# ScalarE's order at the end of the first chunk, and sums and splits made sooner in the second layer, in an adaLN block with a long convolution and a token-mixing MLP

## The chip, the cores and the metric

The kernel runs on one core of a Trainium2 chip. A core has five engines that work at the same time, each through its own list of instructions in order: TensorE (PE in the profile; its weight loads are PEld), VectorE (DVE), ScalarE (ACT), GpSimd (POOL) and SyncE (SP), which here only issues transfers. They meet through semaphores. TensorE writes to PSUM, which TensorE, VectorE and ScalarE reach; the rest of the data on the chip lies in SBUF.

The metric is the device time of one execution in microseconds. Three executions of the kernel before took 678.05, 681.57 and 681.95 us, with a median of 681.57. A fourth, profiled, took 683.93.

## The reference

One batch entry, 2048 tokens, 640 channels, all float32. A condition vector gives six modulation rows of 640. The block has two residual parts. The first normalises each token, modulates it, and multiplies it with the output of a depthwise path: a short causal convolution of `k`, a product with `v`, and a causal convolution as long as the sequence. The second normalises again and runs an MLP over the token axis.

```python
mod = (silu(c) @ w_mod).reshape(1, 6, 1, 640)
sa, ca, ga, sb, cb, gb = mod[:, 0], ..., mod[:, 5]

h = layernorm(x) * (1 + ca) + sa
kv = short_conv(k, shift_k) * v                  # 4 taps, causal, per channel
y = long_conv(kv, ssm_k) + kv * ssm_D            # 2048 taps, causal, per channel (by FFT)
x = x + ga * (h * y)

h = layernorm(x) * (1 + cb) + sb                 # (2048, 640)
u = gelu(einsum("bsd,sf->bdf", h, w1) + b1)      # w1: (2048, 1728)
y = einsum("bdf,fs->bds", u, w2) + b2            # w2: (1728, 2048)
x = x + gb * transpose(y)
```

## The kernel before, in words

**Depthwise path.** The 640 channels are five chunks of 128. For each chunk the long convolution is a two-step transform done as matmuls: `step1` (line 223) forward, on the filter side and on the data side; `f2` (line 242), the second forward step in eight groups, each followed by a ScalarE copy to `kt` (line 246) and two VectorE products (`p`), whose sums GpSimd writes to `Y`; `i2` (line 271) and `i1` (line 291) back. `gate` multiplies the result into the modulated, normalised tokens `A1` on VectorE and adds the product to the tokens on GpSimd.

The work is ordered by hand: the order of the program's lines is the order on each engine. While a chunk is in `f2`, ScalarE also makes the first factors of that chunk, `A1 = x * rstd - mean * rstd`, one activation for each of 16 token groups (the list `ac`, line 298), and VectorE fills its gaps with the short convolution of the chunk after (`kv_ops`, the list `fill`). Chunk 0 is different: the token statistics and the modulation are made at its end, so its 16 factors stand there, after the statistics' square roots (`rstd`, line 335).

**The end of chunk 0** (lines 606 to 637). The modulation's first three rows are a product of `silu(c)` with `w_mod` in five blocks (`mod_part`, line 351) into the PSUM tile `tap`. ScalarE copies the sum to SBUF (`mod_sum`, line 355). TensorE spreads each of three rows over all partitions (`mod_row`, line 362). ScalarE evicts rows 0 and 1 to `G0` and `G1` (lines 369 and 371) and VectorE multiplies row 2 into both. `k0` is ScalarE's eviction of the last `step1` group (line 229). The PSUM tiles of this part turn over three slots, in the order in which they are asked for: row 0, row 1 and row 2 take the slots of the last `i2`'s two tiles and of the last `step1`; the two `i1` tiles take those of rows 0 and 1. Then VectorE applies `G1` and `G0` to the factors (`po`, in two halves, each a multiplication and an addition), ScalarE permutes the next chunk's filter (`perm`, line 168, in two halves), and GpSimd does a quarter of chunk 2's short convolution (`kv_ops(1, pool)`) before the two additions of `gate`.

**First MLP layer.** Weights are split into a high part of a reduced float32 type (`fp32r`, written by ScalarE) and a low rest (VectorE); each product is three matmuls, high by high, high by low, low by high.

**Second MLP layer.** The first four of the 16 output blocks are done plainly (line 1123). The other twelve go in six pairs (`NP = 6`), each pair by seven products in place of eight (a Strassen-Winograd scheme) over the seven combinations

```python
ORDER = ("A11", "A12", "S1", "S2", "S3", "S4", "A22")
```

For the product numbered `n` (7 in a pair, 42 in all): `sums(n)` makes its weight combination on VectorE; it does something only for S1 (one addition), for S2 (two subtractions, which make S3 as well) and for S4 (one). `split(n)` writes the high half on ScalarE (line 1034) and the low half on VectorE into one of three slots, `slots[n % 3]`. `product(n)` is 21 matmuls of 320 columns (line 1046), three for each of seven blocks; the third of each three uses the low half. `outcome(n)` combines the products and, for most, finishes an output half (`finish`: a SCALAR_TENSOR_TENSOR from PSUM, line 1053 or 1055, and one or two TENSOR_TENSOR, then a transfer out). The products' PSUM tiles turn over four slots, which the four plain blocks `acc[0]` to `acc[3]` filled before; `acc[0]` and `acc[1]` are emptied early (`early`, line 1097), `acc[2]` and `acc[3]` by four calls of `finish` in the loop at `n == 1`. The loop (lines 1136 to 1155) runs two splits ahead of the products.

VectorE's and GpSimd's TENSOR_TENSOR instructions all have the line of a helper, 57.

Of the kernel before, what the change touches and what calls it, by code (L numbers as in the profile page):

```python
# [47 lines left out]
def mixer_kernel(ctx: ExitStack, tc: tile.TileContext, q, k, v, shift_k, ssm_k, ssm_D, w1, b1, w2, b2, c,  # L48
# [123 lines left out]
    def taps():  # L172

        act.activation(TAP, TR.rearrange("p (i s) -> p s i", s=4), AF.Copy)
# [183 lines left out]
    def mod_row(i, t, slot=None, later=False):  # L358

        ps, j = psum(slot).rearrange("p (h m) -> p h m", h=2), i % 3  # L360
        for h in range(2):
            pe.matmul(ps[:, h, 0:320], ones[32 * j:32 * j + 1, 0:1].to_broadcast([1, 128]),
                      t[32 * j:32 * j + 1, 320 * h:320 * h + 320], start=True, stop=True)
        ps = ps[:, :, 0:320]
        two = lambda t: t.rearrange("p (h m) -> p h m", h=2)
        if later:
            return lambda: act.activation(two(GB), ps, AF.Copy)
        if i == 0:
            act.activation(two(G0), ps, AF.Copy)
        elif i == 1:  # L370
            act.activation(two(G1), ps, AF.Copy, bias=1.0)
        elif i == 2:
            TT(dve, two(G0), ps, two(G0), ALU.mult)
            TT(dve, two(G1), ps, two(G1), ALU.mult)
        elif i == 3:
            act.activation(two(SB), ps, AF.Copy, accum_out=msb)
        elif i == 4:
            dve.tensor_scalar(two(CB), ps, 1.0, None, op0=ALU.add)
# [98 lines left out]
    def run(ops):  # L477
        for f_ in ops:
            f_()
# [69 lines left out]
    for c in range(NC):  # L549
        cn = c + 1 if c + 1 < NC else None  # L550
        ac, po = a1_ops(c)
# [42 lines left out]
        if c == 0:  # L594
            for kk in range(2, 5):
                mod_load(0, kk, homes[kk])
            step1(0, 0)
            ps = psum()
            pe.transpose(ps[:, 0:36], stg, ID[0:36, 0:36])
            act.activation(cols, ps[:, 0:36], AF.Copy)  # L600
            act.activation(sil, cols[:, 30:35], AF.Silu)
            step1(0, 1)
            i2(0)
            step1(0, 2)
            i2(1)
            k0 = step1(0, 3, True)
            for kk in range(4):
                mod_part(tap, kk, pl[kk])
                if kk == 2:
                    load_D(1)  # L610
                    load_ks(1)
            rstd(rs1, nm1, 0, 16)
            run(ac[0:8])
            k0()
            mod_part(tap, 4, pl[4])
            for o, i in ((0, 2048), (64, 2048)):
                dve.tensor_scalar(T_v1[o:o + 64, i:i + 2048], T_v1[64:128, 0:2048], 1.0, None, op0=ALU.mult)
            dve.tensor_scalar(T_v1[64:128, 0:2048], T_v1[0:64, 0:2048], 1.0, None, op0=ALU.mult)
            load_halo(2)
            load_k(2, 0, n=2)  # L620
            load_v(2, 0, n=2)
            load_k(2, 2, n=2)
            load_v(2, 2, n=2)
            mod_sum(tap, T_kt[:, 0:640])
            run(ac[8:16])
            pool.tensor_scalar(PW, TR.rearrange("p (i s) -> p s i", s=4), 1.0, None, op0=ALU.mult)
            perm_add(1)
            run(kv_ops(1, pool))
            for i in range(3):
                mod_row(i, T_kt[:, 0:640])  # L630
            taps()
            load_taps(3)
            run(po[0:2])
            perm(1)
            load_D(2)
            load_ks(2)
            fill.extend(kv(3, ((0,), (2, 1), (3,))))
        elif cn is not None:
            for t in range(2):
                step1(0, t)  # L640
            perm(cn)
            if c + 2 < NC:
                fill.extend(kv(c + 3 if c + 3 < NC else None))
            else:
                fill.extend(x1s(cc, j) for cc in range(c) for j in range(16))
        else:
            blk.update({f: (j16(t[:, 0:2048]), j16(t[:, 2048:4096])) for f, t in (
                (0, mem("w0", 4096, "wb0")), (1, mem("w1", 4096, "wb1")))})
            mod_load(3, 3, T_z[:, 0:1920])
            mod_load(3, 4, P[:, 0:1920])  # L650
            for kk in range(3):
                mod_part(tap, kk, pl[kk])
            t = mem("in", 4288, "wb3")
            blk[3] = j16(t[:, 0:2048]), j16(t[:, 2048:4096])
            split_rows(0, X, (0, 1, 3))
            split_rows(1, T_aux[:, 0:2048], (0, 1, 3))
            run(po)
# [353 lines left out]
    def sums(n):  # L1011

        p, w_ = n // 7, ORDER[n % 7]
        if p >= NP:
            return
        a = lambda k: A[p, k]
        if w_ == "S1":
            A[p, w_] = S1
            TT(dve, S1, a("A21"), a("A22"), ALU.add)
        elif w_ == "S2":  # L1020
            TT(dve, a("A21"), a("A11"), a("A21"), ALU.subtract)
            TT(dve, a("A11"), S1, a("A11"), ALU.subtract)
            A[p, "S3"], A[p, "S2"] = a("A21"), a("A11")
        elif w_ == "S4":
            TT(dve, a("A12"), a("A12"), a("S2"), ALU.subtract)
            A[p, "S4"] = a("A12")
# [74 lines left out]
    for s in range(NW):  # L1101
        i = NF + s
        acc.append(psum().rearrange("p (h m) -> p h m", h=2))
        split_w(i)
        load_w(i + 1)
        if s < 3:
            t_ops(3 + s)
        if s > 1:
            early(s - 2)
        if s == 3:  # L1110
            load_pair(1, 0, 3)
            m_w.append(mem("w1", 4096, "m_w0"))
            slots += [(q7(m_w[0], 1792 * i), q7(m_w[0], 1792 * i + 896)) for i in range(2)]
            split(0)
            split(1)
            sums(2)
            sums(3)
        wh, wl = blk[i]
        for f_ in range(NF):
            u = U[f_]  # L1120
            for k, (w, r) in enumerate(((wh, 0), (wh, 2), (wl, 0))):
                for h in range(2):
                    pe.matmul(acc[s][:, h, 0:320], w[:, f_].bitcast(F32R), u[r + h].bitcast(F32R),  # L1123
                              start=f_ == 0 and k == 0, stop=f_ == NF - 1 and k == 2)
# [9 lines left out]
    t_ops(6, pool)  # L1134
    load_pair(1, 3, 4)
    for n in range(7 * NP):
        if n:
            sums(n + 3)
        split(n + 2)
        product(n)  # L1140
        if n == 1 or n == 3:
            outcome(n - 1)
        if n != 0 and n != 2:
            outcome(n)
        if n == 1:
            for k in range(4):
                finish(2 + k // 2, k % 2, acc[2 + k // 2][:, k % 2, 0:320], (o2, o4, o3, o1)[k], xq[4 + k])
        if n == 2:
            x_pair(1)
        if n % 7 == 6:  # L1150
            load_pair(n // 7 + 2)
            x_pair(n // 7 + 2)
# [34 lines left out]
```

## Time and profile before

| | |
|---|---|
| timed runs | 678.05, 681.57, 681.95 us; median 681.57 |
| profiled execution | 683.93 us, of which span 682.1 |
| TensorE busy | 629.4 us (92%), weight loads 598.4 |
| VectorE busy | 498.3 us (73%) |
| ScalarE busy | 300.2 us (44%) |
| GpSimd busy | 133.9 us (20%) |
| mean granted TensorE clock | 0.975 |

The stretches in the trace: up to about 103 us chunk 0 and the next chunk's filter; chunks 1 to 4 to about 280; the second normalisation, overlapped with the first products, to about 344; the first MLP layer to 495; the second layer's plain blocks to 544.4; the six pairs to the end.

A row of a timeline has the start in us, the length in us, engine, line, operation, output and inputs by tile name, the shape of the output and of the input, and the count of instructions merged. In square brackets stands how long the engine sat idle just before and what released it. A table by stretch has, after the stretch and its length, the busy time of PE, PEld, DVE, ACT and POOL, each with the count of instructions, then the granted TensorE clock (1.00 is full), the transfers' share of the DMA engines, and GB/s.

### The profile page before, as it was taken

Reading aid. Unit: us, or ns where it says so; the run is one execution under the profiler, and the core shown is the slowest. Engines: PE = TensorE matmul, PEld = TensorE weight load, DVE = VectorE, ACT = ScalarE, POOL = GpSimd, SP = SyncE. Lnnn points to the kernel's source line nnn. Section 1 sums busy time; section 2 is a strip of 40 time slices with the busy share of each in tenths; the row PEclk is TensorE's granted clock in tenths of the full one; section 3 lists DMA queues with packets and bytes.
Section 4 is the critical chain, followed back from the end, with each engine's and each line's share of the span. In section 5 each row is a group of like instructions: output and inputs, shape, how many; then the busy total and the mean of one; then the engine's idle time right before and its main releaser. Section 6 shows DMA issues by size and latency. Waiting matters only on the chain.

```text
span 682.1 us, 20757 instructions
## 1 busy us (share of the span) xinstructions
PE 629.4 (92%) x9119; PEld 598.4 (88%) x9119; DVE 498.3 (73%) x869; ACT 300.2 (44%) x483; POOL 133.9 (20%) x157
## 2 busy tenths in 40 slices
PE   6878778999999898798899999999999989999997
PEld 2877568899989897688899889999999989999997
DVE  7789589989898279798866622321689779888995
ACT  1654655646657265457654222322344133333331
POOL 6762067226134142000000000000000520000000
PEclk9998989999999799888899999999999999999999
DMA  9999797375426153440308333335441634355601
GB/s 188 219 260 274 246 179 157 91 138 121 66 65 215 35 134 104 91 97 1 62 1 154 62 63 63 62 64 115 120 136 55 197 114 124 102 167 166 184 32 38
DMA packets 166538, 81.23 MB, mean 119 GB/s; under 512 B 90830, under 2 KB 156912, under 8 KB 166448
## 3 DMA queue, kind: packets, MB, share of 16 engines
q1 hardware_dynamic: 159276, 78.32, 47.5%
q10 hardware_dynamic: 6916, 1.31, 1.1%
q8 instruction: 71, 1.16, 0.7%
q0 software_dynamic: 256, 0.28, 0.2%
q14 instruction: 19, 0.16, 0.1%
HBM read 69.40 MB, written 10.49 MB: 117 GB/s over the span
## 4 chain that ended last, share of the span: by engine, by line
PE 68%; DVE 14%; ACT 6%; DMA 5%; issue 3%; SPq 2%; POOL 1%; ACTq 0%; POOLq 0%; DVEq 0%
PE pst L445 20%; PE pst L1046 17%; PE pst L1123 7%; PE pst L223 7%; PE pst L242 6%; PE pst L271 5%; PE pst L291 3%; DVE p L57 3%; ACT z L280 2%; DMA in<-in_w_mod_dram 1%; PE pst L919 1%; DVE tap L57 1%; DMA y<-in_A_ssm_k_dram 1%; DVE sm L548 1%; DVE kt L57 1%
## 5 line engine op out<-in xcount | busy, mean ns | idle before, releaser
L242 PE MATMUL pst<-z,w 128*64 128x64 f32 x2560 | 78.4, 223 | 13.1 <-DVE p L57 6.7
L242 PEld LDWEIGHTS pst<-z,w 128*64 128x64 f32 x2560 | 76.4, 138 | 15.6 <-issue 9.1
L229 ACT ACTIVATE z<-pst 128x1024 f32<-128x1024 f32 (+2 forms) x45 | 43.1, 977 | 46.3 <-PE pst L223 46.2
L57 POOL TENSOR_TENSOR y<-p 128x256 f32<-128x256 f32 x72 | 51.3, 741 | 42.4 <-DVE p L57 42.1
L57 DVE TENSOR_TENSOR p<-pst,kt 128x512 f32<-128x512 f32 x80 | 50.7, 680 | 7.9 <-ACT kt L246 7.9
L1046 PE MATMUL pst<-r_z,m_w 128*128 128x320 f32 x222 | 42.0, 312 | 2.2 <-DVE m_w L57 2.2
L882 ACT ACTIVATE pst<-pst,sm 128x640 f32<-128x640 f32 x13 | 10.0, 767 | 75.9 <-PE pst L445 75.9
L271 PEld LDWEIGHTS pst<-v,y 32*128 32x128 f32 x1280 | 38.2, 187 | 5.4 <-issue 4.8
L271 PE MATMUL pst<-v,y 32*128 32x64 f32 x1280 | 40.1, 272 | 2.5 <-issue 2.3
L246 ACT ACTIVATE kt<-pst 128x512 f32<-128x512 f32 x40 | 24.0, 599 | 34.6 <-PE pst L242 18.7
L1034 ACT ACTIVATE m_w<-m_v 128x896 fp32r<-128x896 f32 x24 | 22.7, 951 | 36.9 <-PE pst L1046 16.8
L223 PE MATMUL pst<-v,x 128*64 128x128 f32 x512 | 34.6, 291 | 4.5 <-issue 4.0
L223 PE MATMUL pst<-v,p 128*64 128x128 f32 x640 | 36.7, 274 | 0.8 <-ACT p L168 0.8
L1046 PEld LDWEIGHTS pst<-r_z,m_w 128*128 128x128 f32 x222 | 35.2, 190 | 2.4 <-DVE m_w L57 2.4
L57 POOL TENSOR_TENSOR m_p<-u_i,r_z 128x320 f32<-128x320 f32 x1 | 0.9, 875 | 183.4 <-issue 183.4
L223 PEld LDWEIGHTS pst<-v,p 128*64 128x64 f32 x640 | 34.8, 137 | 2.1 <-ACT p L168 1.7
L57 DVE TENSOR_TENSOR tap<-tap,kt 128x512 f32<-128x512 f32 x51 | 35.5, 696 | 1.3
L223 PEld LDWEIGHTS pst<-v,x 128*64 128x64 f32 x512 | 31.1, 147 | 5.8 <-issue 5.2
L291 PEld LDWEIGHTS pst<-z,v 64*64 64x64 f32 x1280 | 23.9, 156 | 9.1 <-issue 3.8
L280 ACT ACTIVATE z<-pst 128x512 f32<-128x512 f32 x38 | 20.9, 647 | 23.3 <-PE pst L271 23.3
L291 PE MATMUL pst<-z,v 64*64 64x64 f32 x1280 | 25.3, 241 | 6.3 <-issue 2.4
L57 DVE TENSOR_TENSOR kt<-in,tap 128x512 f32<-128x512 f32 x42 | 28.8, 685 | 1.2
(308 smaller groups left out, 1507.4 us busy)
## 6 DMA issues: line engine op xcount, KB each, us to landing
x<-in_B_w_dram SPq DMA_DIRECT2D x20, 512.0 KB
m_x<-xs SPq DMA_DIRECT2D x28, 160.0 KB
out_dram<-m_x SPq DMA_DIRECT2D x28, 160.0 KB
aux<-in_A_ssm_k_dram SPq DMA_DIRECT2D x8, 512.0 KB
m_v<-in_B_w_dram SPq DMA_DIRECT2D x9, 448.0 KB
in<-in_w_mod_dram SPq DMA_DIRECT2D x4, 960.0 KB
x<-in_B_w_dram SPq DMA_DIRECT2D x7, 448.0 KB
in<-in_A_v_dram SPq DMA_DIRECT2D x22, 128.0 KB
```

The lines of the kernel that those rows point to most:

```text
L57: TT = lambda eng, o, a, b, op: eng.tensor_tensor(o, a, b, op=op)
L223: pe.matmul(ps[64 * ri:64 * ri + 64, o:o + 255:2], lhs, F1[:, 128 * ri:128 * ri + 128], start=True, stop=True)
L229: act.activation(Z[:, side, t, :, k0:k1], ps.rearrange("p (a k e) -> p a k e", a=4, e=2)[:, :, k0:k1], AF.Copy)
L242: pe.matmul(ps[64 * h:64 * h + 64, o:o + 64], W2[k1 // 32][:, 2 * (k1 % 32) + ri], rhs, start=True, stop=True)
L246: act.activation(kt.rearrange("p (m i) -> p m i", i=32), pv[:, :, 1], AF.Copy)
L271: pe.matmul(pp[qd // 2][:, o:o + 64], Y[p, ri, i:i + 2].rearrange("p i k -> p (i k)"), V2[p, 64 * ri:64 * ri + 64], start=ri == 0, stop=ri ...
L280: act.activation(o, i, AF.Copy)
L291: pe.matmul(ps[64 * b:64 * b + 64, 512 * e + 64 * jj:512 * e + 64 * jj + 64], V1[p, ri, n2], T2[p, :, 32 * ri + n2], start=ri == 0, stop=r ...
L445: pe.matmul(ps[0:m, h, 0:320], w_.bitcast(F32R), r_[:, 320 * h:320 * h + 320].bitcast(F32R), start=first and i == 0, stop=last and i == 2)
L1034: act.activation(W[n][0].bitcast(F32R), A[p, w_], AF.Copy)
L1046: pe.matmul(bank[n], w[:, i].bitcast(F32R), r.bitcast(F32R), start=i == 0 and k == 0, stop=i == 6 and k == 2)
L1123: pe.matmul(acc[s][:, h, 0:320], w[:, f_].bitcast(F32R), u[r + h].bitcast(F32R), start=f_ == 0 and k == 0, stop=f_ == NF - 1 and k == 2)
```

## The change

At the end of chunk 0, ScalarE's list is reordered. Before: eight factors, the `step1` eviction `k0`, the copy of the modulation's sum, eight factors, the evictions of rows 0 and 1. After: four factors, the copy of the sum, `k0`, the evictions of rows 0 and 1, twelve factors. What the other engines have in their lists stays in its order.

In the second layer, the S4 combination of the first pair (`sums(5)`) is made before the loop, beside S1 and S2, instead of at `n == 2`. In the loop's first turns, `split(4)` moves from the top of `n == 2` to `n == 1`, between `outcome(0)` and `outcome(1)`; the four `finish` calls are parted, two at `n == 1` and two at `n == 2`; and `split(5)` moves from the top of `n == 3` to `n == 2`, ahead of the second two. The calls of `sums` left out for `n == 1` do nothing in either kernel. No arithmetic, tile or transfer is added or taken away.

```diff
@@ -610,8 +610,7 @@
             rstd(rs1, nm1, 0, 16)
-            run(ac[0:8])
-            k0()
+            run(ac[0:4])
             mod_part(tap, 4, pl[4])
...
@@ -622,12 +621,13 @@
             mod_sum(tap, T_kt[:, 0:640])
-            run(ac[8:16])
+            k0()
             pool.tensor_scalar(PW, TR.rearrange("p (i s) -> p s i", s=4), 1.0, None, op0=ALU.mult)
             perm_add(1)
             run(kv_ops(1, pool))
             for i in range(3):
                 mod_row(i, T_kt[:, 0:640])
+            run(ac[4:16])
             taps()
...
@@ -1113,8 +1113,8 @@
             split(0)
             split(1)
-            sums(2)
-            sums(3)
+            for n in (2, 3, 5):
+                sums(n)
...
@@ -1134,16 +1134,21 @@
     for n in range(7 * NP):
-        if n:
+        if n > 2:
             sums(n + 3)
-        split(n + 2)
+        if n not in (2, 3):
+            split(n + 2)
         product(n)
         if n == 1 or n == 3:
             outcome(n - 1)
+        if n == 1:
+            split(4)
         if n != 0 and n != 2:
             outcome(n)
-        if n == 1:
-            for k in range(4):
+        if n == 2:
+            split(5)
+        if n in (1, 2):
+            for k in (2 * n - 2, 2 * n - 1):
                 finish(2 + k // 2, k % 2, acc[2 + k // 2][:, k % 2, 0:320], (o2, o4, o3, o1)[k], xq[4 + k])
         if n == 2:
             x_pair(1)
```

## The prediction, on record before the result

> **What bounds the kernel now.** I read the page first for the span and the chain of waits, then the timelines of the two stretches that the diff touches, engine by engine, and last the table by stretch for the granted clock.
>
> ```profile
> span 682.1 us, 20757 instructions
> PE 68%; DVE 14%; ACT 6%; DMA 5%; issue 3%; SPq 2%; POOL 1%; ACTq 0%; POOLq 0%; DVEq 0%
> ```
>
> TensorE carries 68% of the chain that ended last. So an edit pays where TensorE waits. The end of the second layer's lead-in is such a place. TensorE's timeline there:
>
> ```profile
> 556.74 0.45 PE L1046 MATMUL pst<-r_z,m_w 128*128 128x320 f32 x2
> 559.36 0.43 PE L1046 MATMUL pst<-r_z,m_w 128*128 128x320 f32 x1 [2.17 <-DVE m_w L57]
> 563.80 1.49 PE L1046 MATMUL pst<-u_i,m_w 128*128 128x320 f32 x9
> 569.96 1.04 PE L1046 MATMUL pst<-u_t,m_w 128*128 128x320 f32 x6
> ```
>
> A product of the second layer is 21 matmuls. Products 5 and 6 fill 563.80 to 569.96, so 3.08 us each. Product 4 fills 556.74 to 563.80, 7.06 us, so 3.98 us are lost: after two matmuls it waits 2.17 us in the record for the low half of its own split, from VectorE, and then runs slowly. The table by stretch (PE, PEld, DVE, ACT, POOL busy with counts, then the granted clock, DMA share, GB/s) shows the slowness as clock, here and in two stretches of the first chunk's end:
>
> ```profile
> 88.00:94.00 6.00, 5.54 (x246) 5.40 (x247) 5.83 (x6) 3.04 (x4) 2.23 (x3) 0.67 1.25 200
> 94.00:97.00 3.00, 1.08 (x24) 1.01 (x25) 2.86 (x3) 0.00 (x0) 2.92 (x2) 1.00 1.12 196
> 559.40:563.80 4.40, 4.40 (x19) 4.40 (x20) 2.49 (x3) 1.14 (x2) 0.00 (x0) 0.61 0.40 130
> ```
>
> 19 matmuls take 4.40 us there; 19/21 of 3.08 is 2.79, so the clock of 0.61 costs 1.6 us. Call that the price of one cold stretch.
>
> **Second layer, the cause.** VectorE's and then ScalarE's timeline:
>
> ```profile
> 548.91 1.24 DVE L57 TENSOR_TENSOR m_w<-m_p,m_w 128x896 fp32r<-128x896 f32 x1 [7.26 <-ACT m_w L1034]
> 550.08 1.76 DVE L57 TENSOR_TENSOR m_w<-m_v,m_w 128x896 fp32r<-128x896 f32 x1
> 551.76 0.54 DVE L1055 SCALAR_TENSOR_TENSOR m_x<-pst,sm,m_x 128x320 f32<-128x320 f32 x1
> ...
> 553.27 0.55 DVE L1053 SCALAR_TENSOR_TENSOR m_x<-pst,sm,rows 128x320 f32<-128x320 f32 x1
> ...
> 557.22 1.08 DVE L57 TENSOR_TENSOR m_v<-m_v 128x896 f32<-128x896 f32 x1
> 558.22 2.27 DVE L57 TENSOR_TENSOR m_w<-m_v,m_w 128x896 fp32r<-128x896 f32 x2
> 560.41 0.48 DVE L57 TENSOR_TENSOR m_x<-pst,m_x 128x320 f32<-128x320 f32 x1
> ...
> 574.61 1.08 DVE L57 TENSOR_TENSOR m_w<-m_p,m_w 128x896 fp32r<-128x896 f32 x1
> ```
> ```profile
> 551.12 0.94 ACT L1034 ACTIVATE m_w<-m_v 128x896 fp32r<-128x896 f32 x1
> 558.42 0.95 ACT L1034 ACTIVATE m_w<-m_v 128x896 fp32r<-128x896 f32 x1 [6.36 <-DVE m_v L57]
> ```
>
> The high half of split 4 was written at 551.12 to 552.06. Its low half came only with the pair at 558.22 (ready about 559.3), because VectorE had ahead of it outcome 1 (551.76 to 553.27, 1.51 us), four finishes (to 557.22, 0.99 us each) and the S4 sum (1.08 us). The change does the S4 sum in front of the loop, where VectorE idles 7.26 us: nothing, and if that idle were not there, 1.08 us. It puts split 4 ahead of outcome 1 and split 5 between the finishes, two and two.
>
> The new order on VectorE: split 3 ends 551.8, waits for ScalarE until 552.1 (0.3 idle, new), split 4 to 553.1, outcome 1 to 554.6, two finishes to 556.6, split 5 to 557.6, two finishes to 559.6. ScalarE's high half of split 5 need not wait for S4 any more, only for its slot, free when product 2 ends (556.74 - 3.08 = 553.66). TensorE: product 4 at 556.74 finds its low half 3.6 us old. The finishes that are now queued behind the two splits empty the PSUM tiles that products 4 and 5 write into; the second finish's PSUM read ends at about 556.2 (555.6 + 0.55), the fourth's at 559.2, for products that start at 556.74 and 559.82. That is only about 0.5 us of room, but it is room. All 3.98 us go.
>
> What is late next: with TensorE 4 us sooner, VectorE's backlog. From 548.91 to the end of split 9's low half (574.61 + about 1.1) it was idle just once, 2.1 us before outcome 4, waiting for the late product. Less S4, that is 26.8 - 2.1 - 1.1 = 23.6 us of work, plus the new 0.3: done at 572.8. Product 9 would start at 556.74 + 5 x 3.08 = 572.14 and need it two matmuls on, at 572.4. So a stall of about 0.4 us there; it is between 0 and, with 1 us of mistake in the order, 1.4. Second layer: 3.98 - 0.4 = 3.6 us gained.
>
> **First chunk's end.** ScalarE, then TensorE:
>
> ```profile
> 79.44 3.19 ACT L298 ACTIVATE aux<-xa,sm 128x128 f32<-128x128 f32 x8 [1.60 <-DVE sm L340]
> 82.53 1.02 ACT L229 ACTIVATE z<-pst 128x1024 f32<-128x1024 f32 x1
> 83.45 0.67 ACT L355 ACTIVATE kt<-tap 96x640 f32<-96x640 f32 x1
> 84.03 3.17 ACT L298 ACTIVATE aux<-xb,sm 128x128 f32<-128x128 f32 x8
> 87.11 0.68 ACT L369 ACTIVATE g<-pst 128x640 f32<-128x640 f32 x1
> ...
> 88.84 2.20 ACT L168 ACTIVATE p<-aux 128x1024 f32<-128x1024 f32 x2
> ```
> ```profile
> 80.15 1.25 PE L351 MATMUL tap<-p,sm 128*32 128x320 f32 x12
> ...
> 84.17 1.61 PE L362 MATMUL pst<-kt,sm 1*128 1x320 f32 x12 [2.77 <-ACT kt L355]
> 87.83 5.71 PE L291 MATMUL pst<-z,v 64*64 64x64 f32 x246 [2.05 <-ACT g L369]
> 95.92 0.39 PE L291 MATMUL pst<-z,v 64*64 64x64 f32 x10 [2.38 <-issue]
> 96.24 7.21 PE L223 MATMUL pst<-v,p 128*64 128x128 f32 x128
> ```
>
> The modulation's product ends at 81.40, but ScalarE copies its sum (L355) at 83.45, behind eight factors and one eviction, and evicts the rows (L369) behind eight more. TensorE waits 2.77 and 2.05 us for these. New order: four factors to 81.0; the sum, now waited for, 81.45 to 82.05; the z eviction to 82.97; rows 0 and 1 to 84.15; twelve factors at 0.40 us to 88.9; taps; the permutation 89.5 to 91.7. The added wait is 0.4 us of ScalarE with everything else queued behind it; so the permutation ends at 91.7 instead of 91.04. Row 2's matmuls reuse the PSUM slot that the z eviction empties, now only after the sum: needed about 83.2, free 82.97.
>
> TensorE's inverse transform (L291) then starts at 83.6, 4.2 us sooner. It has 5.71 us, at full clock 5.71 x 0.67 = 3.8, and the 2.38 us stall that the profile calls issue, so it ends between 90 and 92. Its next step (L223) needs the permutation's first half, at 90.6. Against 96.24 that is some 4 to 5.5 us. VectorE:
>
> ```profile
> 87.81 1.55 DVE L57 TENSOR_TENSOR g<-pst,g 128x640 f32<-128x640 f32 x2 [4.67 <-ACT g L369]
> 89.40 2.48 DVE L57 TENSOR_TENSOR aux<-aux,g 128x1024 f32<-128x1024 f32 x2
> ...
> 93.13 3.41 DVE L57 TENSOR_TENSOR aux<-aux,g 128x1024 f32<-128x1024 f32 x2
> ...
> 97.79 0.69 DVE L57 TENSOR_TENSOR tap<-in,tap 128x512 f32<-128x512 f32 x1
> ...
> 109.96 1.28 DVE L57 TENSOR_TENSOR p<-pst,kt 128x512 f32<-128x512 f32 x2
> ```
>
> Its modulation rows run 83.8 to 85.4, the first pair waits for the eighth factor (85.75) to 88.2, the gate 89.5, the second pair 92.0, the gate 93.2: 4.6 us sooner than 97.79. But these are not the last to arrive. GpSimd, and ScalarE's first factors of the next chunk:
>
> ```profile
> 91.92 3.54 POOL L57 TENSOR_TENSOR t<-in,t 128x512 f32<-128x512 f32 x2 [3.77 <-DMA in<-in_A_k_dram]
> ...
> 97.78 1.27 POOL L57 TENSOR_TENSOR t<-in,t 128x512 f32<-128x512 f32 x1
> ...
> 104.45 2.37 POOL L57 TENSOR_TENSOR xa<-xa,aux 128x1024 f32<-128x1024 f32 x1
> ```
> ```profile
> 106.86 0.88 ACT L298 ACTIVATE aux<-xa,sm 128x128 f32<-128x128 f32 x2 [0.18 <-POOL xa L57]
> 107.94 0.60 ACT L246 ACTIVATE kt<-pst 128x512 f32<-128x512 f32 x1 [0.20 <-PE pst L242]
> ```
>
> GpSimd starts on a load that no edit moves (its issues on SP stand behind TensorE and other loads alone), at 91.92, and its gate addition ends at 106.82. The next chunk's factors overwrite what that addition reads, and behind them on ScalarE stands the copy (107.94 to 108.54) for VectorE's second multiplication. If GpSimd kept its time, that multiplication would come at 108.5 against 109.96: 1.4 us gained. But three GpSimd operations from 91.92 to 97.78 took 5.86 us, where three of 1.27 with gaps of 0.09 make 4.08: they were stretched by 1.78 while VectorE's second pair, with both inputs in SBUF, took 3.41 in place of 2.48. In the new order that pair is over at 92.0. So the addition ends at 105.04, the copy ends as before 1.68 us after the first factor starts, at 106.74, and the multiplication gains 109.96 - 106.74 = 3.2 us. From there VectorE paces the chunk, its fills of the next chunk done at the old spacing. Nothing paced by a load follows soon, so I carry 3.2 on; bounds 0 and 4.6.
>
> **The sum.** 3.6 + 3.2 = 6.8 us. The profiled execution took 683.93 us, its span and 1.8 us around it, above all three timed runs (median 681.57). 683.93 - 6.8 = 677.1; the same gain taken from the median, 681.57 - 6.8, is 674.8 us, which I forecast.
>
> **A rule on the clock.** Row: 2.17 us of waiting was followed by 0.61, 2.77 and 2.05 (at 84.17 and 87.83) by 0.67, and 2.38 (95.92) by 1.00. The Trainium skill ("TensorE: Matmul & The Clock Gate", Part 1) says that the clock halves after an idle window of about 3.4 us, in windows that run freely. By that rule a 2.17 us wait is too short, the slow stretch isn't its doing, and the sum would be 1.6 us less, 5.2. The trace's two slow stretches after shorter waits speak against it.
>
> **The rivals.**
> *The slow clock stays*: the cold stretch at 559.4 has another cause, or comes again at product 9's stall. Then 1.6 us of the second layer stay lost: 674.8 + 1.6 = 676.4. For it: one wait of 2.38 us cooled nothing. Against: at 563.80 to 569.96, without a wait, the products run at 3.08.
> *GpSimd stays the bound*: its stretching has another cause or only moves. First chunk 1.4: 674.8 + 1.8 = 676.6.
> *The first part does nothing*: the issue stall at 93.54 falls where it fell in time, not in work, so L223 again starts near 96.2: 674.8 + 3.2 = 678.0. For it, loads fill the DMA share to 1.25 in 88 to 94 in either order; against it, a stall in L291 now lies before the permutation is done.
> *Neither part does what it says*: the late halves are then held by slots, not by order, and the time is 681.6. Against: ScalarE wrote split 4's high half at 551.12, so its slot was free.
> *Slower*: the clock gate through the chunks and the layer norms. Each wait of 2 us or so cools the clock or not, as the rows show, and everything after 90 us is shifted against it. Each further cold stretch costs 1.6; from the fifth (6.8/1.6 = 4.3) the change loses: five give 682.8, nine 689.2. For it: the same wait had both outcomes in one trace. Against: shifted waits should gain as often as they lose, and where VectorE paces, a slow TensorE is covered.
>
> **How the numbers follow.** Forecast 0.60 (own range 672 to 677: product 9's bounds, the gate additions' bounds and one cold stretch either way); slow clock 0.12, GpSimd 0.12, first part nothing 0.07, neither 0.04, slower 0.05. Low end 671: 674.8 less the 0.4, less the 1.4 that VectorE's 4.6 has over 3.2, less one cold stretch. High end 679.5: the first part's nothing, plus one cold stretch; beyond it lie neither and slower and little more. A measurement tells about 1% from no change, so the line is 681.57 x 0.99 = 674.75, on which the forecast lies: faster takes 0.30 of its 0.60 and 0.08 of the other cases' lower sides, 0.38; slower by over 1%, above 688.4, is the tail of the last rival, 0.03; the rest, 0.59, lies within 1%.
>
> **What would show it.** Products 4 and 5 in TensorE's timeline at 3.08 us each, clock 1.00 there, no wait on VectorE; split 4's low half ahead of the SCALAR_TENSOR_TENSOR of outcome 1; at most a short wait at product 9. The copy from tap at 81.5, the row eviction at 83.0, L291 at 83.6. GpSimd's first three operations at 1.3 us each, its xa addition ending at 105, VectorE's second multiplication of the next chunk at 106.7. A wait of products 4 or 5 for a finish, a GpSimd addition that still ends at 106.8, or a gain that is there at 125 us and gone at 340 would prove me wrong.

## The result, and the profile after

Eleven executions of the changed kernel have a median of 677.59 us (675.72 to 680.65); eleven of the kernel before, beside them, 681.83 us (678.05 to 683.80). The ratio is 0.9938 with a 95% interval of 0.9915 to 0.9961: 4.2 us or 0.6% less. That lies within 1% of no change, and the interval leaves out no change itself. The time falls inside the predicted range of 671.0 to 679.5, but the gain is 4.2 us where the prediction summed 6.8.

The profiled execution of the changed kernel took 675.72 us, the lowest of its eleven; that of the kernel before, 683.93, lies above all of its eleven. So the spans below differ by 8.2 us, twice what the change is worth, and one trace against one trace can't give the size of a part. (In two of the kernels below, the first chunk's edits alone in their first run and the changed kernel with little GpSimd work, the profiled execution was a disturbed one, and its trace isn't read.) The page's span and chain after:

```profile
span 673.9 us, 20760 instructions
PE 67%; DVE 16%; ACT 6%; issue 4%; DMA 3%; SPq 2%; POOL 1%; ACTq 0%; DVEq 0%; POOLq 0%
```

**The second layer.** TensorE's timeline after, at the starts of products 0, 4, 5, 6, 7 and at product 9:

```profile
539.82 1.04 PE L1046 MATMUL pst<-u_t,m_w 128*128 128x320 f32 x6
...
552.14 0.60 PE L1046 MATMUL pst<-r_z,m_w 128*128 128x320 f32 x3
...
555.22 1.48 PE L1046 MATMUL pst<-u_i,m_w 128*128 128x320 f32 x9
...
558.30 0.60 PE L1046 MATMUL pst<-r_z,m_w 128*128 128x320 f32 x3
...
561.38 1.04 PE L1046 MATMUL pst<-u_t,m_w 128*128 128x320 f32 x6
...
567.54 1.44 PE L1046 MATMUL pst<-r_z,m_w 128*128 128x320 f32 x6
```

Products 4 (552.14 to 555.22) and 5 (555.22 to 558.30) take 3.08 us each, and all seven of the first pair 561.38 - 539.82 = 21.56, seven times 3.08. No wait is left before product 9, whose first six matmuls take 1.44 in place of 1.04. VectorE's timeline after:

```profile
537.09 1.09 DVE L57 TENSOR_TENSOR m_v<-m_v 128x896 f32<-128x896 f32 x1
...
547.49 1.09 DVE L57 TENSOR_TENSOR m_w<-m_v,m_w 128x896 fp32r<-128x896 f32 x1 [0.24 <-ACT m_w L1034]
548.50 0.55 DVE L1055 SCALAR_TENSOR_TENSOR m_x<-pst,sm,m_x 128x320 f32<-128x320 f32 x1
...
552.00 1.08 DVE L57 TENSOR_TENSOR m_w<-m_v,m_w 128x896 fp32r<-128x896 f32 x1
...
553.99 0.54 DVE L1053 SCALAR_TENSOR_TENSOR m_x<-pst,sm,rows 128x320 f32<-128x320 f32 x1
```

The S4 sum stands at 537.09, ahead of the loop. The low half of split 4 (547.49) is written ahead of outcome 1 (548.50), after a new wait of 0.24 us for ScalarE; split 5's (552.00) comes between the finishes.

**The end of the first chunk.** VectorE's last instruction of the statistics, then ScalarE's and TensorE's timelines after:

```profile
77.59 0.18 DVE L340 SCALAR_TENSOR_TENSOR sm<-sm 128x16 f32<-128x16 f32 x1
...
107.06 1.29 DVE L57 TENSOR_TENSOR p<-pst,kt 128x512 f32<-128x512 f32 x2 [1.87 <-ACT kt L246]
```
```profile
77.81 1.65 ACT L298 ACTIVATE aux<-xa,sm 128x128 f32<-128x128 f32 x4 [1.58 <-DVE sm L340]
81.51 0.70 ACT L355 ACTIVATE kt<-tap 96x640 f32<-96x640 f32 x1 [2.05 <-PE tap L351]
82.11 1.03 ACT L229 ACTIVATE z<-pst 128x1024 f32<-128x1024 f32 x1
83.64 0.70 ACT L369 ACTIVATE g<-pst 128x640 f32<-128x640 f32 x1 [0.50 <-PE pst L362]
...
105.67 0.88 ACT L298 ACTIVATE aux<-xa,sm 128x128 f32<-128x128 f32 x2 [4.04 <-POOL xa L57]
```
```profile
72.35 3.49 PE L223 MATMUL pst<-v,x 128*64 128x128 f32 x32
...
80.20 1.25 PE L351 MATMUL tap<-p,sm 128*32 128x320 f32 x12
82.26 2.27 PE L362 MATMUL pst<-kt,sm 1*128 1x320 f32 x12 [0.82 <-ACT kt L355]
84.46 3.84 PE L291 MATMUL pst<-z,v 64*64 64x64 f32 x246
89.39 0.44 PE L291 MATMUL pst<-z,v 64*64 64x64 f32 x10 [1.09 <-issue]
91.20 7.21 PE L223 MATMUL pst<-v,p 128*64 128x128 f32 x128 [1.37 <-ACT p L168]
```

ScalarE makes four factors and then waits 2.05 us for the modulation's product. The prediction had 0.45 there. The reason stands three lines above in TensorE's own list: the data side's last forward step takes 3.49 us here. In the trace that the prediction was made from it took 1.97, as its row and the granted clock (the third number from the end of a row of the table by stretch) show. First the kernel before: TensorE's timeline, VectorE's, and the table by stretch. Then the table of the changed kernel:

```profile
73.92 1.97 PE L223 MATMUL pst<-v,x 128*64 128x128 f32 x32
```
```profile
79.22 0.18 DVE L340 SCALAR_TENSOR_TENSOR sm<-sm 128x16 f32<-128x16 f32 x1
```
```profile
73.92:75.82 1.90, 1.90 (x35) 1.73 (x32) 0.00 (x0) 1.80 (x4) 0.00 (x0) 1.00 1.04 399
```
```profile
72.35:75.77 3.42, 3.42 (x36) 3.09 (x33) 0.65 (x3) 3.31 (x5) 0.00 (x0) 0.54 1.04 396
```

The clock is 1.00 in the one and 0.54 in the other, for the same matmuls in the same place, which no edit touches.

### The profile page after: what moved, and what is told of

The parts are those of the page before. It is cut to its first block, busy times and chain, and to the rows that moved or that the text cites. A ratio compares the mean times of both kernels' runs of the same rounds, so it can differ in the third digit from the quotient of the medians.

```text
span 673.9 us, 20760 instructions
## 1 busy us (share of the span) xinstructions
PE 628.9 (93%) x9119; PEld 596.1 (88%) x9119; DVE 497.5 (74%) x869; ACT 300.1 (45%) x483; POOL 133.5 (20%) x157
## 4 chain that ended last, share of the span: by engine, by line
PE 67%; DVE 16%; ACT 6%; issue 4%; DMA 3%; SPq 2%; POOL 1%; ACTq 0%; DVEq 0%; POOLq 0%
PE pst L445 20%; PE pst L1046 16%; PE pst L1123 7%; PE pst L223 7%; PE pst L271 6%; PE pst L242 6%; DVE p L57 2%; PE pst L291 2%; ACT z L280 2%; DVE tap L57 2%; PE tap L351 2%; PE pst L919 1%; DVE kt L57 1%; DMA y<-in_A_ssm_k_dram 1%; DVE aux L57 1%
## 5 line engine op out<-in xcount | busy, mean ns | idle before, releaser
L57 DVE TENSOR_TENSOR m_w<-m_v,m_w 128x896 fp32r<-128x896 f32 x24 | 27.9, 1165 | 2.5 <-ACT m_w L1034 2.1
L445 PE MATMUL pst<-r_z,wb0b 128*128 128x320 f32 x180 | 28.2, 310 | 0.9 <-DVE u_x L57 0.9
```

The source lines that it names most:

```text
L57: TT = lambda eng, o, a, b, op: eng.tensor_tensor(o, a, b, op=op)
L445: pe.matmul(ps[0:m, h, 0:320], w_.bitcast(F32R), r_[:, 320 * h:320 * h + 320].bitcast(F32R), start=first and i == 0, stop=last and i == 2)
```

## The experiments

Each ran beside the kernel before on the same chip; ratios are to that.

### The kernel before and the changed kernel, once more

Both unchanged.

> The kernel before, unchanged, to see how far two executions of one kernel differ stage by stage. Every theory: ratio 1.000, within 0.3%. Theory A (both parts give what was forecast, but the one profiled execution of before was a slow one, above all other executions): the traces of before differ by some microseconds ahead of the second layer, and product 4 loses between 2.3 us (the wait alone) and 4.0 us (wait and slow clock). Theory B (the first part's gain is given back later): this trace has the same stage lengths as the first, product 4 losing 4.0 us.

> The changed kernel, unchanged. Every theory: ratio 0.994, about 4.2 us faster. Theory A: stage lengths ahead of the second layer vary by 2 us or more between its two traces; products 4 and 5 take 3.08 us each in both. Theory B: the lead of the first chunk's end, some 3 us at VectorE's second multiplication of chunk 1, is in both traces smaller by the start of the first MLP layer.

Before: 680.58 us against 682.14 for the same program beside it, ratio 0.9975 (0.9948 to 1.0001). So such a comparison can be off by a quarter of a per cent, 1.6 us, and nothing smaller is read from any of these. After: 677.78, 0.9940 (0.9912 to 0.9968), as the first time.

The second trace of the kernel before differs from the first in just the two places on which the prediction's prices rest. TensorE's timeline, the table by stretch and ScalarE's copy:

```profile
73.24 3.46 PE L223 MATMUL pst<-v,x 128*64 128x128 f32 x32
...
80.96 1.25 PE L351 MATMUL tap<-p,sm 128*32 128x320 f32 x12
...
558.40 0.42 PE L1046 MATMUL pst<-r_z,m_w 128*128 128x320 f32 x1 [2.18 <-DVE m_w L57]
...
561.29 1.48 PE L1046 MATMUL pst<-u_i,m_w 128*128 128x320 f32 x9
```
```profile
73.24:76.63 3.39, 3.39 (x36) 3.22 (x33) 0.00 (x0) 3.29 (x5) 0.00 (x0) 0.54 1.04 395
558.40:561.29 2.89, 2.89 (x19) 2.89 (x20) 2.49 (x3) 1.18 (x3) 0.00 (x0) 1.00 0.63 194
```
```profile
82.69 0.69 ACT L355 ACTIVATE kt<-tap 96x640 f32<-96x640 f32 x1
```

Here the forward step is slow, and the modulation's product ends at 82.21, only 0.5 us before ScalarE's old list reaches the copy. And the wait at product 4, 2.18 us, is followed by full speed (1.00) where the first trace had 0.61.

The times below are counted from the start of VectorE's last statistics instruction (L340), because that itself comes between 77.06 and 80.03 us for reasons ahead of the change. Each entry is a difference of two starts, or of an end and a start.

| trace | forward step at 72 to 75 us takes | modulation's product ends | copy of the sum | L291 starts | GpSimd's addition to `xa` ends | VectorE's second multiplication, next chunk |
|---|---|---|---|---|---|---|
| before | 1.97 | 2.18 | 4.23 | 8.61 | 27.60 | 30.74 |
| before, again | 3.46 | 3.74 | 4.22 | 8.62 | 29.16 | 30.58 |
| second layer's edits only | 3.39 | 3.68 | 4.24 | 8.64 | 28.34 | 30.40 |
| after | 3.49 | 3.86 | 3.92 | 6.87 | 28.05 | 29.47 |
| after, again | 3.68 | 4.14 | 4.20 | 7.15 | 28.31 | 29.74 |
| first chunk's edits only | 3.41 | 3.68 | 3.74 | 6.68 | 28.21 | 30.07 |

The copy is 0 to 0.5 us sooner in the new order, not 2. L291 is 1.5 to 1.9 us sooner, not 4.2. At VectorE's second multiplication some 0.8 us is left: the mean of the first three is 30.57, of the last three 29.76. GpSimd's addition ends 0.2 us sooner in the mean (28.37 and 28.19), not the 1.78 us of the forecast.

### Each part alone

The first chunk's edits without the second layer's, run twice, and the second layer's without the first chunk's.

```diff
# the first chunk's edits alone (against the changed kernel)
-            for n in (2, 3, 5):
-                sums(n)
+            sums(2)
+            sums(3)
...
-        if n > 2:
+        if n:
             sums(n + 3)
-        if n not in (2, 3):
-            split(n + 2)
+        split(n + 2)
...
-        if n == 1:
-            split(4)
...
-        if n == 2:
-            split(5)
-        if n in (1, 2):
-            for k in (2 * n - 2, 2 * n - 1):
+        if n == 1:
+            for k in range(4):
```
```diff
# the second layer's edits alone (against the changed kernel)
-            run(ac[0:4])
+            run(ac[0:8])
+            k0()
...
-            k0()
+            run(ac[8:16])
...
-            run(ac[4:16])
```

> Only the first chunk's end reordered, the second layer as before. Forecast's own term: 3.2 us faster, ratio 0.9953. Theory B (given back later): 0 to 1 us faster, ratio 0.9985 to 1.000. Theory C (the first part carries, the second part's 3.6 us is mostly a slow clock that other executions do not have): 3 us faster or more, ratio 0.9955.

> Only the first chunk's end reordered, once more, for its time and for a trace with the second layer as before. By the traces so far (the lead at VectorE's second multiplication 1.2 us, not 3.2): 1.2 to 2.5 us faster, ratio 0.9965 to 0.998. Product 4 waits 2.2 us for VectorE; whether its matmuls then run at a granted clock of 1.00 (as in the second trace of before, loss 2.4 us) or 0.6 (as in the first, loss 4.0) is open: the theory that the slow clock belongs to the wait says 0.6, the theory that it hangs on when the wait falls allows both.

> Only the second layer's sums, splits and finishes moved, the first chunk as before. Forecast's own term: 3.6 us faster, ratio 0.9947. Theory B: 3.6 us, and with the whole change at 4.2 the first part gives 0.6. Theory C: 1 to 2 us, ratio 0.997 to 0.9985, because product 4 loses its wait of 2.2 us but usually no slow clock, and product 9 takes back 0.4.

First chunk alone: 680.68, ratio 0.9967 (0.9945 to 0.9989), and 681.82, 0.9990 (0.9963 to 1.0016), so 2.3 and 0.7 us, 1.5 as a mean. Second layer alone: 680.57, 0.9973 (0.9946 to 1.0000), 1.8 us with an interval of 0.0 to 3.7. The two add to 3.3, the whole gained 4.1 and 4.2: within what these intervals allow, the parts add, but neither part alone is clearly more than the 1.6 us by which one program differed from itself.

The traces size the second layer better than the times, since nothing else moves its products against each other. From product 0 to product 7 takes 21.56 us in all seven traces with the new order there; with the old one it takes 25.53 or 25.54 in four traces (the kernel before's first, the first chunk's edits alone, and two of the kernels below) and 24.00 in one (the kernel before, again). Less the 0.4 us that product 9 loses in the new order, the gain is 3.6 us in four of five and 2.0 in the fifth, 3.3 as a mean. What the mean is over more executions is open: five are few. The gain is kept to the end: from product 0 to the end of the span takes 137.7 and 136.2 us in the two traces of the kernel before and 134.1 in both of the changed kernel.

### Is GpSimd what holds the next chunk?

In the changed kernel ScalarE waits 4.04 us for GpSimd's gate addition (above, 105.67). If GpSimd sets the end there, making it free should bring the rest of the forecast. Six of the eight GpSimd operations ahead of the gate additions left out (chunk 2's short convolution is then incomplete in that quarter), in the changed kernel and in the kernel before:

```diff
-            run(kv_ops(1, pool))
+            o_ = kv_ops(1, pool)
+            run([o_[0], o_[-1]])
```

> The changed kernel with GpSimd's part of chunk 2's short convolution cut from eight operations to two (the first product and the last are kept; the three other taps are left out for that quarter). If GpSimd's two gate additions, behind that convolution, hold the next chunk's factors and with them VectorE's second multiplication: in the trace the xa addition ends some 8 us sooner (about 98), ScalarE's first factors of chunk 1 wait no longer, the second multiplication comes at 105 instead of 107 to 108, and the start of chunk 1's last part (the matmuls on x after its eight groups) comes 2 to 3 us sooner; about 2 us faster than the changed kernel, ratio to before 0.991. If GpSimd isn't the bound: no more than 0.5 us.

> The kernel before with the same six operations of GpSimd left out. If the first chunk's end is bound there by TensorE and VectorE and not by GpSimd: VectorE's second multiplication moves by under 0.5 us; its second pair on the factors (3.4 us, stretched beside GpSimd) may shorten by up to 0.9; ratio 0.999 to 1.000. If GpSimd bounds this kernel as well: 2 us faster, ratio 0.997.

And, in the changed kernel, nothing left out, but chunk 1's factors made one group later, so that the copy for VectorE doesn't stand behind GpSimd:

```diff
-                for f_ in ac[2 * g:2 * g + 2]:
+                for f_ in (ac[2 * g:2 * g + 2] if c > 1 else ac[max(2 * g - 2, 0):2 * g if g < 7 else 16]):
```

> The changed kernel with chunk 1's factors on ScalarE one group later (none beside group 0, four beside group 7), so that the copy for VectorE's second multiplication no longer stands behind a factor that waits for GpSimd. If that wait is what holds the first part's gain: the second multiplication at 105.3 instead of 107 to 108; the third is then held by GpSimd's first sum (end at 109.3), so that 0.9 to 1 us is left; ratio to before 0.9925. If it is not: same as the changed kernel, 0.994.

After with little GpSimd work: 677.93, ratio 0.9933 (0.9903 to 0.9962); before with it: 683.10, 1.0000 (0.9974 to 1.0026); factors later: 677.52, 0.9927 (0.9903 to 0.9951). None differs from its own kernel by more than the intervals, which are some 1.6 to 2 us wide to either side: a gain of 1 us would not show, and the 0.9927 of the factors made later is nearer to what was expected if they were in the way (0.9925) than to the other case (0.994). In the kernel before with little GpSimd work, GpSimd's and VectorE's timelines:

```profile
96.86 2.37 POOL L57 TENSOR_TENSOR xa<-xa,aux 128x1024 f32<-128x1024 f32 x1
```
```profile
106.91 1.29 DVE L57 TENSOR_TENSOR p<-pst,kt 128x512 f32<-128x512 f32 x2 [1.94 <-ACT kt L246]
...
110.17 1.28 DVE L57 TENSOR_TENSOR p<-pst,kt 128x512 f32<-128x512 f32 x2
```

The addition is over at 99.2, 7.6 us sooner than in the kernel before, and VectorE's second multiplication comes at 110.17 (109.96 before). ScalarE's timeline with the factors later, and VectorE's:

```profile
105.39 0.60 ACT L246 ACTIVATE kt<-pst 128x512 f32<-128x512 f32 x1 [1.37 <-PE pst L242]
107.26 0.60 ACT L246 ACTIVATE kt<-pst 128x512 f32<-128x512 f32 x1 [1.27 <-PE pst L242]
```
```profile
106.02 1.29 DVE L57 TENSOR_TENSOR p<-pst,kt 128x512 f32<-128x512 f32 x2 [2.21 <-ACT kt L246]
...
109.28 1.28 DVE L57 TENSOR_TENSOR p<-pst,kt 128x512 f32<-128x512 f32 x2
```

With GpSimd out of the way, ScalarE's copies wait 1.37 and 1.27 us for TensorE's groups, and VectorE for the first copy. But TensorE is late in this trace for a reason that the edit doesn't touch: L291 stands twice in waits called issue, 1.37 and 2.73 us, where the changed kernel's first trace has 1.09. So GpSimd is the last to arrive in both traces of the changed kernel, where VectorE's second multiplication waits 1.87 and 1.61 us and starts 1.42 and 1.43 after the end of GpSimd's addition; and TensorE's chain can be last instead, as here and in the trace of the first chunk's edits alone, where VectorE's first multiplication waits 2.67 us for a copy that TensorE's chain leads to, and the second follows it without a wait. How much freeing GpSimd is worth in a usual execution these runs don't show.

### Is the modulation's product what holds the copy?

All five blocks of the product moved ahead of the data side's last forward step, in the changed kernel and in the kernel before:

```diff
-            k0 = step1(0, 3, True)
-            for kk in range(4):
+            for kk in range(5):
                 mod_part(tap, kk, pl[kk])
...
+            k0 = step1(0, 3, True)
             rstd(rs1, nm1, 0, 16)
...
-            mod_part(tap, 4, pl[4])
```

> The changed kernel with TensorE's modulation product (five blocks) ahead of the last forward step of the data side instead of behind it. If in most executions the sum's copy in the changed kernel waits for TensorE, because that forward step runs at a slow clock (3.4 us in place of 1.97 in eight of nine traces): the product ends 3 us sooner, the copy stands 1.7 to 2.0 us after the statistics (VectorE's line 340) in place of 3.7 to 4.2, the inverse transform starts 4.5 to 5.0 us after them in place of 6.7 to 7.2, and the kernel is 1 to 2 us faster than the changed one, ratio to before 0.991 to 0.9925. If the copy's place isn't what holds the gain: same as the changed kernel, 0.994.

> The kernel before with the same move of TensorE's product. There ScalarE's list holds the copy (eight factors and an eviction ahead of it, 4.2 us after the statistics in four traces of four), so the earlier product changes nothing in it: copy at 4.2, the eviction perhaps later as its step now comes last; ratio 0.999 to 1.001. If TensorE held the copy there as well: 1 us or more faster.

In the changed kernel: 677.77, ratio 0.9926 (0.9896 to 0.9955), where 1 to 2 us less than the changed kernel were expected; that it is better than without the move (0.9938 and 0.9940) isn't shown. Its statistics end with VectorE's instruction at 77.95; ScalarE's timeline, and TensorE's:

```profile
80.18 0.70 ACT L355 ACTIVATE kt<-tap 96x640 f32<-96x640 f32 x1 [0.37 <-PE tap L351]
82.06 1.04 ACT L229 ACTIVATE z<-pst 128x1024 f32<-128x1024 f32 x1 [1.18 <-PE pst L223]
```
```profile
84.42 3.84 PE L291 MATMUL pst<-z,v 64*64 64x64 f32 x246
```

The copy now comes 2.23 us after the statistics, with a wait of 0.37: what the prediction had for the changed kernel itself. But the `z` eviction between it and the rows now waits 1.18 us for the step that was moved back, and L291 starts 6.47 after the statistics, 0.4 sooner than in the changed kernel. Row 2 needs the slot that this eviction empties, so the two can't simply change places. VectorE's second multiplication comes 28.67 after the statistics, 0.8 and 1.1 sooner than in the two traces of the changed kernel, with GpSimd's addition over at 26.56.

In the kernel before no change was expected; the median is 684.34, 1.0037 (1.0011 to 1.0063), a loss little larger than one program's difference from itself. TensorE's timeline and ScalarE's:

```profile
80.75 2.02 PE L351 MATMUL tap<-p,sm 128*32 128x320 f32 x12 [2.37 <-DMA p<-in_w_mod_dram]
```
```profile
85.60 1.02 ACT L229 ACTIVATE z<-pst 128x1024 f32<-128x1024 f32 x1 [3.88 <-PE pst L223]
86.52 0.69 ACT L355 ACTIVATE kt<-tap 96x640 f32<-96x640 f32 x1
```

The last block of `w_mod` landed late in this execution, the forward step stood behind it, and in the old order the copy stands behind the eviction of that step. This execution took 688.83, 4.5 us above the median, so it shows how the move can lose and not how much it usually does.

### Which half of the first chunk's edit pays?

The second layer's edits kept, and ScalarE's first eight factors, eviction and copy as before; only the last eight factors go behind the rows:

```diff
# against the changed kernel
-            run(ac[0:4])
+            run(ac[0:8])
+            k0()
...
             mod_sum(tap, T_kt[:, 0:640])
-            k0()
...
-            run(ac[4:16])
+            run(ac[8:16])
```

> The changed kernel with the front of ScalarE's list as it was (eight factors, the eviction, then the sum's copy); only the evictions of rows 0 and 1 stay ahead of the last eight factors. If moving the copy ahead is worth 0.1 to 0.5 us, because TensorE's product ends about when the old list reaches the copy: the copy 4.2 us after the statistics, the inverse transform 6.6 to 7.2 after them, as in the changed kernel (6.7 to 7.2) and not 8.6 as before; ratio to before as the changed kernel, 0.994. If the copy's move carries the gain, as forecast (2.0 of its 4.2 us): inverse transform at 8.0 or later, ratio 0.9955 or more.

679.16 (eight executions), ratio 0.9934 (0.9900 to 0.9969), as good as the changed kernel. The statistics end with the instruction at 80.03; ScalarE's timeline, and TensorE's:

```profile
84.27 0.68 ACT L355 ACTIVATE kt<-tap 96x640 f32<-96x640 f32 x1
86.37 0.70 ACT L369 ACTIVATE g<-pst 128x640 f32<-128x640 f32 x1 [1.43 <-PE pst L362]
```
```profile
87.12 5.51 PE L291 MATMUL pst<-z,v 64*64 64x64 f32 x256 [0.76 <-ACT g L369]
```

The copy is where the old order has it, 4.24 after the statistics, and L291 starts at 7.09, between the two traces of the changed kernel (6.87 and 7.15). What the first chunk gains comes from the rows going ahead of the last eight factors; that the sum goes ahead of four factors and the eviction adds nothing that shows. The execution behind this trace took 683.25 us, 4.1 above the median of its kernel; where it lost its lead is told below, under the sum.

### All the moves together

The changed kernel with the product first, the factors later, and in the second layer's loop the split ahead of the sums, for product 9:

```diff
# beside the two edits above, against the changed kernel
-        if n > 2:
-            sums(n + 3)
         if n not in (2, 3):
             split(n + 2)
+        if n > 2:
+            sums(n + 3)
```

> The changed kernel with TensorE's product first, chunk 1's factors one group later on ScalarE, and in the second layer each split ahead of the sums of its turn (product 9 no longer waits for a low half: 0.4 us). By what each is good for: the first 1 to 2 us; the second now pays, since TensorE is earlier and GpSimd's addition would hold the second multiplication, up to 1 us; the third 0.4. Together 2 to 3.5 us faster than the changed kernel, ratio to before 0.989 to 0.991. If the gains are lost in the later chunks: 0.993.

675.83, ratio 0.9908 (0.9883 to 0.9934), the best of all, 6.3 us under the kernel before beside it. Its interval overlaps that of the changed kernel (0.9915 to 0.9961), so that it is the better of the two isn't shown. TensorE at product 9:

```profile
566.66 1.04 PE L1045 MATMUL pst<-r_z,m_w 128*128 128x320 f32 x6
```

1.04 us in place of 1.44: the split ahead of the sums takes product 9's loss away, and products 0 to 13 take 582.06 - 538.94 = 43.12 us against 43.5 in the other traces of the new order.

## Why the prediction was right or wrong

**Second layer: right, by its steps and nearly by its size.** The cause (split 4's low half behind outcome, finishes and S4), the new order, 3.08 us for products 4 and 5 and the 0.4 us at product 9 all came as written; ScalarE's 0.3 us ahead of split 4 measured 0.24, and no product waited for a finish. Of the 3.6 us, the 1.6 for the cold stretch isn't there every time: the wait was 2.17 or 2.18 us in all five traces of the old order, and a slow stretch followed in four. So the gain is 3.6 or 2.0, with a mean of 3.3. *The slow clock stays* was half true: the cold stretch did go with the wait, but in some executions there was none to remove.

**First chunk: the sign right, the size wrong.** The step that failed is "the sum, now waited for, 81.45 to 82.05" in place of 83.45, and with it L291's "starts at 83.6, 4.2 us sooner". It took the end of the modulation's product, 81.40, from a trace in which the forward step ahead of it happened to run at full clock. In the eight other traces with that order on TensorE the step takes 2.9 to 3.7 us instead of 1.97, and the product ends 3.7 to 4.1 us after the statistics instead of 2.2. The old list reaches the copy at 4.2. So about 2 of the 4.2 us were never there to gain; the wait only changed from TensorE's (2.77 us for the copy) to ScalarE's (2.05 for the product). The row eviction's part, 1.5 to 1.9 us, was there.

**What came behind it.** The term that stands in the prediction's sum, 3.2 us, failed at the step "the addition ends at 105.04", 1.78 us sooner. GpSimd's operations were less stretched, as forecast, but not freed: from 91.92 to 97.78 before, and after

```profile
91.77 3.37 POOL L57 TENSOR_TENSOR t<-in,t 128x512 f32<-128x512 f32 x2 [3.81 <-DMA in<-in_A_k_dram]
...
96.57 1.29 POOL L57 TENSOR_TENSOR t<-in,t 128x512 f32<-128x512 f32 x1
...
103.25 2.39 POOL L57 TENSOR_TENSOR xa<-xa,aux 128x1024 f32<-128x1024 f32 x1
```

that is 4.80 us in place of 5.86, where 4.08 was forecast: VectorE's second pair moved less far than expected and still met the first of them. The addition ended at 105.64 (forecast 105.04), VectorE's second multiplication came at 107.06 (forecast 106.74). This near hit is partly luck: the statistics came 79.22 - 77.59 = 1.6 us sooner in this trace, which no edit does.

Counted from the statistics, the multiplication gained 0.8 us on average, not 3.2, and GpSimd's addition 0.2. The three operations do take less in the new order (4.80, 4.37 and 3.95 us in its three traces of the table, against 5.86, 5.64 and 5.79), but they start later after the statistics: 14.2 to 15.2 us, against 12.7 to 14.5. The load that they wait for hangs on the forward step too: an issue of SyncE that stands ahead of it (L157) waits 4.8 us for a block of the modulation's product (`tap`, L351) in the kernel before and 5.2 in the changed one, and goes on 0.1 us after the statistics in the trace with the fast step and 1.6 to 2.0 in the other five of the table. That fits the early GpSimd of the first trace, the 12.7; whether the edits move the load at all, beyond the scatter of these traces, is open.

*GpSimd stays the bound* named the right engine in both traces of the changed kernel and would have given 1.4 us; but freeing GpSimd gained nothing that these runs can measure, and in two other traces of the new order TensorE's chain was last, so it is one of two bounds, and which one holds differs between executions. *The first part does nothing* has its stall in fact, 1.09 us called issue before the last ten matmuls of L291, after the work as before and not at a fixed time (2.98 us in the changed kernel's second trace, 1.77 to 2.38 in the three of the old order); the first part does less than forecast for the reason above, not for this one.

**The sum.** 3.3 and 0.8 make 4.1, and 4.2 and 4.1 were measured. That agreement is better than its terms deserve. At product 0 of the second layer the traces with the first chunk's edits alone or with the whole change (three) reach it 3.1 us sooner after the statistics than those without (four), single pairs between 1.5 and 5.2, while the timed runs give the first part 0.7 and 2.3 us. In the six traces of the table the mean lead at the start of L291 in chunks 1 to 4 is 0.8, 1.4, 2.0 and 2.8 us: it grows chunk by chunk. But the trace with only the rows ahead is 1.2 us ahead of the old order's mean in chunk 1 and 2.7 behind it in chunk 3, and reaches product 0 later (467.3 us after the statistics) than any of those four (465.0 to 466.2). So executions scatter by as much as the lead, and what makes it grow is open.

**Two errors have one source.** The one profiled execution had a step at full clock at 73.92, which put the modulation's product too early, and a cold stretch at 559.36, which put the wait's price at the upper of its two values (the commoner one, four of five). Both made the change look better. The prediction did take the gain from the median rather than from that execution's time, which kept the level right.

**Slower** did not happen: of the further cold stretches that it needed, none shows up in the second layer's lead-in, and the mean granted clock after is 0.979 (0.975 before).

## What to carry to other kernels

Before a wait is priced, look at whether the instruction it waits for ran at its usual speed in that execution: one more profile of the same kernel would have shown 3.46 us for the step that read 1.97, and taken 2 us out of the 4.2 that were forecast for TensorE's start. Moving work earlier on the engine that is late is worth nothing where the input comes from another engine just in time; what paid was to let TensorE's input go ahead of work that nobody waits for. And when a wait is removed and another appears in its place (GpSimd's 4.04 us), test it by removing that one too before calling it the bound, and look at more than one trace: here the next bound was GpSimd in some executions and TensorE in others.

## What the runs showed of the hardware

The clock after a short wait is not set by the wait's length alone. At product 4 the same wait, same instructions and same place gave the row quoted above with 1.00, 0.61 in the prediction's table, and in the kernel with the first chunk's edits alone

```profile
558.43 0.42 PE L1046 MATMUL pst<-r_z,m_w 128*128 128x320 f32 x1 [2.17 <-DVE m_w L57]
```
```profile
558.43:562.87 4.44, 4.43 (x19) 4.44 (x20) 2.49 (x3) 1.18 (x3) 0.00 (x0) 0.62 0.41 132
```

0.62. The forward step at 72 to 75 us, 1 to 2 us behind a wait called issue of 1.5 to 2.6 us, was granted 0.50 to 0.65 in eight traces and 1.00 in one; that one came behind the shortest of these waits, 1.49, so there the length may matter, where at product 4 waits of 2.17 and 2.18 us can't be told apart by it. Such a stretch costs about 1.5 us at product 4 (25.53 less 24.00) and 0.95 to 1.71 at the forward step (2.92 to 3.68 against 1.97). The Trainium skill ("TensorE: Matmul & The Clock Gate", Part 1) has the clock follow activity in windows of some 3.4 us that run freely, so that the same kernel differs from run to run. The scatter agrees with that; that it takes an idle window of 3.4 us doesn't agree with waits of 2.2 us after which the clock fell in four traces of five.
